# Routing's intermediate values in spare PSUM columns, and the first expert's raw weights loaded four units later

## The chip, the cores and the metric

The kernel runs on one core of a Trainium2 chip. Its engines are TensorE (PE in the profile; PEld is its weight load), VectorE (DVE), ScalarE (ACT), GpSimd (POOL) and SyncE (SP, which only issues DMA transfers here). The metric is the device time of one execution in microseconds (us), as the median of several runs.

## The reference

Three layers follow each other: causal attention over 4 batches, 12 heads, 448 tokens and a head size of 64; a layer of 8 experts, each token going to one; and a dense layer with `h - tanh(h)` between its two products.

```python
scores = scale * np.matmul(q, k.transpose(0, 1, 3, 2))
scores = np.where(mask, -1000000000.0, scores)
attn = np.exp(scores - np.max(scores, axis=-1, keepdims=True))
attn = attn / (np.sum(attn, axis=-1, keepdims=True) + 1e-09)
x = np.matmul(attn, v)                       # (4,12,448,64) -> (1792, 768)

logits = x @ w_gate                          # 8 experts
e_idx = np.argmax(logits, axis=1)
gate_w = softmax(logits)[arange, e_idx]
eom = 1.0 / (1.0 + np.exp(-(x @ w_output_gate)))
for e in range(8):
    out[mask_e] = gate_w * eom[:, e] * (np.maximum(x[mask_e] @ w1[e], 0.0) @ w2[e])

h = out @ w_in
return (h - np.tanh(h)) @ w_out
```

## The kernel before

The program runs the three layers one after the other, with the weights of the next expert loaded and converted meanwhile. Every engine runs its own instructions in the order in which the code writes them down; semaphores make an instruction wait for those of other engines that it depends on. Two engines' uses of one PSUM bank are ordered by such waits too, whichever columns of the bank they touch.

**Attention** is cut into 24 units (NU): unit u is one batch and a pair of heads. A loop runs over u, and inside it over six steps m = 0 to 5 (L607). In each step stand instructions of several units: scores of unit u (`s_mm`, L328 and L329, with the high and the low half of the keys, kh and kl), their row minimum on DVE (`s_max`, L335), the exponential on ACT (`s_exp`), the transposes of unit u-1 (`t_mm`, `t_out`), the product with v of unit u-2 (`v_mm`, L380), its scaling (`v_out`), the split of the result in two 16-bit halves on POOL and its store (`x_out`, `x_store`), the transposes of unit u-3 (`g_mm`, L429) and the router's logits of unit u-4 (`g_lg`, `g_add`). The product with v is made for two heads; head 0 is written in steps 0 to 2 and head 1 in steps 3 to 5. Each head's product lies in one PSUM bank of the pool `ps_o`, which has two banks and is used by the two heads in turn.

**Inputs of the attention.** Two units share one set of inputs, z = u // 2. At step 4 of unit 2z-4, `load_unit(z)` issues a converting load t16 on POOL's queue (L291, `t<-kq` in the trace) and the 32-bit load of q and k and of v on SP's queue (L251, L252, into parts of raw1 or raw2). At step 3 of unit 2z-2, `rest(0)` copies t16 into kh and qa (L300, L301), makes the low half lo for the first unit's heads on POOL (L302) and issues lo's copies into qa and kl (L303, L305); at step 0 of unit 2z-1, `rest(1)` does the second unit's heads. There is one buffer lo, so POOL's L302 of the next z waits for the last kl copy of this z.

**The first expert's w1** has six row blocks k. Block k is loaded into raw1[:, k % 2] on SP's queue at the head of an odd unit (L610) and converted by `conv1` in steps 2 to 4 two units later: two halves on ACT (L115), the rest on POOL (L117 and L131, two of each). The blocks of the second expert's w1 follow into raw1 at units 18 to 23 (`W1_NEXT`, L590).

**Routing** of a batch of 448 tokens begins when the last logits of the batch are summed in `lga`, in step 2 of units 9, 15, 21 and 27. It is a generator whose parts run in steps 0, 2 and 4, each after the attention's instructions of the step: lg (L453, sum of two parts of lga), mx, ex, eq (L462, L463), the one-hot choice oh (L466, L468), the rank among earlier tokens rkm (L495, L496), its quotient and rest pi and pf (L503 to L506), the weight (L473 to L482, with an exponential of es on ACT, L476), and the masks bi, ba and bb for the token list. All these are tiles of [112, 4 to 64] values in the SBUF pool `sm`.

Lines of the change: pools L238 and L239, `v_mm` L371, `routing` L451, `W1_NEXT` L590, the loads L609 and the conversions L671.

Of the kernel before, what the change touches and what calls it, by code (L numbers as in the profile page):

```python
# [12 lines left out]
F32 = mybir.dt.float32  # L13
F16 = mybir.dt.float16
BF16 = mybir.dt.bfloat16
I32 = mybir.dt.int32
# [4 lines left out]
PSUM = bass.MemoryType.PSUM  # L21
SP = mybir.EngineType.SP

B, H, S, D = 4, 12, 448, 64
CP, NCH = 112, 4
NT, DM = B * S, H * D
E, F1 = 8, 1024
F2 = 2048
KD, KF1, KF2 = DM // 128, F1 // 128, F2 // 128
# [30 lines left out]
def build(ctx: ExitStack, tc: tile.TileContext, kq0, kq, v, wg, wo, w1, w2, wf, out):  # L60
    nc = tc.nc
# [33 lines left out]
    raw1 = raw_p.tile([128, KD, F1], F32, name="raw1")  # L95
# [85 lines left out]
    with ExitStack() as actx:  # L181
# [3 lines left out]
        sm = sctx.enter_context(tc.tile_pool(reuse_waits="tile", name="sm", bufs=3, side="right"))  # L185
# [52 lines left out]
        ps_t = actx.enter_context(tc.tile_pool(reuse_waits="tile", name="ps_t", bufs=3, space=PSUM))  # L238
        ps_o = actx.enter_context(tc.tile_pool(reuse_waits="tile", name="ps_o", bufs=2, space=PSUM))  # L239

# [69 lines left out]
        NU = B * 6  # L310
# [60 lines left out]
        def v_mm(u, h, i):  # L371
            d = st_[u]
            hl = (u % 2) * 2 + h
            if ("o", h) not in d:
                d["o", h] = ps_o.tile([128, 512], F32, tag="o", name=f"o_{u}_{h}")[:CP, 0 : NCH * (D + 1)].rearrange(
                    "p (c d) -> p c d", c=NCH)
            po = d["o", h]
            for j in range(i + 1):
                g, o = where[(h, i, j)]
                nc.tensor.matmul(out=po[:, i, :], lhsT=d["PT"][:, g, o : o + CP], rhs=d["t"][3][:, hl, j, :], start=(j == 0),  # L380
                                 stop=(j == i))
# [69 lines left out]
        def routing(b):  # L451
            lg = sm.tile([CP, NCH, 2 * E], F32, tag="lg", name=f"lg_{b}")
            nc.vector.tensor_tensor(out=lg, in0=lga[:, :, 2 * E :], in1=lga[:, :, 0 : 2 * E], op=ALU.add)  # L453
# [6 lines left out]
            nc.scalar.activation(out=ex, in_=ex, func=AF.Exp, scale=1.0 / LSC)  # L460
            eq = sm.tile([CP, NCH, E], F32, tag="eq", name=f"eq_{b}")
            nc.vector.tensor_tensor(out=eq, in0=lg[:, :, 0:E], in1=mxb, op=ALU.is_equal)  # L462
# [8 lines left out]
            def weight():  # L471
                eo = sm.tile([CP, NCH, E], F32, tag="eo", name=f"eo_{b}")
                nc.vector.tensor_tensor(out=eo, in0=lg[:, :, E:], in1=ohb, op=ALU.mult)  # L473
                es = sm.tile([CP, NCH, 1], F32, tag="es", name=f"es_{b}")
                nc.vector.tensor_reduce(out=es, in_=eo, op=ALU.add, axis=AX.X)
                nc.scalar.activation(out=es, in_=es, func=AF.Exp, scale=-1.0 / LSC)  # L476
                sx = sm.tile([CP, NCH, 1], F32, tag="sx", name=f"sx_{b}")
                nc.vector.tensor_reduce(out=sx, in_=ex, op=ALU.add, axis=AX.X)
                yield
                nc.vector.tensor_scalar(out=es, in0=es, scalar1=1.0, scalar2=YSC, op0=ALU.add, op1=ALU.mult)  # L480
                nc.vector.scalar_tensor_tensor(out=es, in0=sx, scalar=1e-9, in1=es, op0=ALU.add, op1=ALU.mult)
                nc.vector.reciprocal(out=tm[:, b * NCH : (b + 1) * NCH, 1:2], in_=es)  # L482
                yield
# [7 lines left out]
            for c in range(NCH):  # L491
                nc.tensor.matmul(out=prv[:, c + 1 :, :], lhsT=onesb[:CP, :CP],
                                 rhs=oh[:, b, c : c + 1, :].to_broadcast([CP, NCH - c, E]), start=False, stop=(c == NCH - 1))
            rk = sm.tile([CP, NCH, E], F32, tag="rk", name=f"rkm_{b}")
            nc.vector.tensor_tensor(out=rk, in0=prv[:, 0:NCH, :], in1=base.unsqueeze(1).to_broadcast([CP, NCH, E]), op=ALU.add)  # L495
# [4 lines left out]
            yield  # L500
            pi = sm.tile([CP, 3, NCH], I32, tag="pi", name=f"pi_{b}")
            pf = sm.tile([CP, 2, NCH], F32, tag="pf", name=f"pf_{b}")
            nc.vector.tensor_copy(out=pi[:, 0, :], in_=rb)  # L503
# [87 lines left out]
        RS, LD = ((3, 0), (0, 1)), (4, 0)  # L591
        W1_NEXT = {NU - KD + j: k for j, k in enumerate((0, 1, 5, 2, 3, 4))}
        CONV = {(NU - 3, 3): (4,), (NU - 2, 3): (5,), (NU - 2, 5): (6,), (NU - 1, 3): (7,), (NU, 3): (0,), (NU, 5): (1,), (NU + 1, 1): (2,), (NU + 1, 4): (3,)}

        def conv1(k, z):
            raw, hi, lo = raw1[:, k % 2], wts0[0][:, 0, k], wts0[0][:, 1, k]
            if z < 2:
                h = slice(512 * z, 512 * (z + 1))
                scaled("a", hi[:, h], raw[:, h])
            else:  # L600
                rest_of("p", lo, raw, hi)
# [5 lines left out]
        for u in range(NU + 5):  # L607
            if ok(u):
                if u % 2 and 3 <= u < 15:  # L609
                    nc.sync.dma_start(out=raw1[:, (u // 2 - 1) % 2], in_=w1[0, :, u // 2 - 1])  # L610
                if u in (8, 10, 12, 14):
# [16 lines left out]
            for m in range(6):  # L628
# [40 lines left out]
                if u == 4 and m == 0:  # L669
                    wts0 = w_tiles(0)  # L670
                if u % 2 and 5 <= u < 17 and 2 <= m < 5:  # L671
                    conv1((u - 5) // 2, m - 2)
                for k in CONV.get((u, m), ()):
# [793 lines left out]
```

## Time and profile before

| what | value |
|---|---|
| median of 3 runs (lowest, highest) | 1032.12 us (1030.98, 1037.31) |
| the profiled execution | 1036.02 us, span 1034.3 us |
| mean granted TensorE clock | 0.982 of full speed |
| PE busy | 981.5 us (95%) |
| DVE, ACT, POOL busy | 785.0, 604.1, 467.3 us |
| attention stage | about 7 to 225 us |

The profile is of one execution. It gives each engine's busy time, the granted clock of TensorE (1.00 is 2.4 GHz, 0.50 is 1.2 GHz), the share of the 16 DMA engines in use, and a timeline in which an instruction that had to wait carries the idle time ahead of it and what ended that time, as `[2.59 <-DMA kl<-lo]`. Times in it count from the span's start.

### The profile page before, as it was taken

What the parts mean: (1) busy time and instruction counts of PE and PEld (TensorE: products, weight loads), DVE (VectorE), ACT (ScalarE), POOL (GpSimd) and SP (SyncE); (2) the same over time, 40 slices, a digit from 0 to 9 for tenths busy, and PEclk for the clock granted to TensorE, in tenths of its full rate; (3) what the DMA queues carried; (4) which work ended last, traced back from release to release, by engine and by line L of the source; (5) the groups of instructions that cost most, each with busy time, mean ns of one, the idle gap of its engine ahead of it and who ended that gap; (6) DMA issues with size and microseconds to landing.
All of it is one profiled execution on the core that took longest, in us unless ns stands there. A gap on an engine that the chain in (4) does not pass through costs nothing. (4 is left out here: it accounts for less than half of the span.)

```text
span 1034.3 us, 23797 instructions
## 1 busy us (share of the span) xinstructions
PE 981.5 (95%) x8985; PEld 735.5 (71%) x8985; DVE 785.0 (76%) x1704; ACT 604.1 (58%) x1213; POOL 467.3 (45%) x504
## 2 busy tenths in 40 slices
PE   5989999999899998998998899999999999999996
PEld 3989999988678786686876455666666666667763
DVE  6647878787887778668886999887888798776640
ACT  5658887765456365564334698565556566555530
POOL 5466776575211021122136689645544443443321
PEclk9979999999999999999999999999999999999999
DMA  8888999954998988988986360010000000000000
GB/s 244 232 200 232 268 263 224 258 188 144 327 338 333 359 277 303 339 295 300 323 321 220 130 273 1 31 40 16 23 32 31 8 32 8 16 16 16 16 24 23
DMA packets 62648, 173.94 MB, mean 168 GB/s; under 512 B 8368, under 2 KB 23344, under 8 KB 59424
## 3 DMA queue, kind: packets, MB, share of 16 engines
q1 hardware_dynamic: 56352, 147.20, 42.5%
q0 software_dynamic: 6144, 24.84, 8.7%
q8 instruction: 80, 1.31, 0.5%
q14 instruction: 72, 0.59, 0.2%
HBM read 132.30 MB, written 29.62 MB: 157 GB/s over the span
## 5 line engine op out<-in xcount | busy, mean ns | idle before, releaser
L1361 PE MATMUL fo<-wo,g 128*128 128x384 f16 x1344 | 228.2, 326 | 0.0
L1310 PEld LDWEIGHTS <-raw 128*128 128x128 f16 x1440 | 141.2, 98 | 86.7 <-issue 9.0
L1361 PEld LDWEIGHTS <-g 128*128 128x128 f16 x1344 | 131.2, 98 | 83.8
L1320 POOL TENSOR_TENSOR V<-cu,cc 128x384 f32<-128x384 f32 (+1 forms) x80 | 80.1, 1001 | 188.0 <-ACT cu L1319 185.4
L164 PEld LDWEIGHTS <-w 128*128 128x128 f16 x2592 | 146.0, 98 | 9.5 <-issue 8.1
L1310 PE MATMUL fh<-cu,raw 128*128 128x384 f16 (+1 forms) x864 | 133.1, 310 | 4.6 <-DVE cc L1318 3.4
L380 PE MATMUL o<-v,PT 112*112 112x65 f32 x960 | 119.4, 266 | 0.0
L343 ACT ACTIVATE P<-s,nb 112x112 f32<-112x112 f32 (+1 forms) x192 | 89.8, 495 | 49.5 <-DVE nb L335 24.9
L380 PEld LDWEIGHTS o<-v,PT 112*112 112x112 f32 x960 | 110.3, 185 | 0.2
L123 DVE SCALAR_TENSOR_TENSOR w<-raw,w 128x768 f16<-128x768 f32 (+1 forms) x99 | 99.0, 1060 | 11.4 <-ACT w L115 11.4
L335 DVE CUSTOM_DVE_ANT_0 s<-s,maskw 112x112 f32<-112x112 f32 (+1 forms) x192 | 85.8, 459 | 21.4 <-PE s L329 18.4
L811 POOL DMA_INDIRECT xg<-xs_d,idx x22 | 30.7, 1397 | 155.9 <-PEq L886 36.5
L1319 ACT ACTIVATE cu<-cc 128x384 f32<-128x384 f32 (+1 forms) x80 | 40.0, 500 | 93.9 <-DVE cc L1318 93.9
L115 ACT ACTIVATE w<-raw 128x768 f16<-128x768 f32 (+2 forms) x106 | 89.4, 904 | 6.7 <-DMA raw<-w 3.9
L1318 DVE TENSOR_TENSOR cc<-fh,co 128x384 f32<-128x384 f32 (+1 forms) x80 | 42.0, 525 | 63.5 <-PE fh L1310 50.8
L1323 POOL TENSOR_TENSOR X<-cc,X 128x384 f32<-128x384 f32 (+1 forms) x80 | 87.6, 1094 | 4.1 <-ACT X L1322 0.5
L1330 DVE SCALAR_TENSOR_TENSOR V<-cu,V 128x384 f32<-128x384 f32 (+1 forms) x80 | 82.6, 1032 | 0.1
L1338 DVE TENSOR_TENSOR V<-V,co 128x384 f32<-128x384 f32 (+1 forms) x64 | 77.5, 1211 | 0.0
L361 PE MATMUL t<-ident,P 112*112 112x112 f32 x480 | 69.3, 268 | 0.0
L1310 PE MATMUL fh<-yh,raw 128*128 128x384 f16 x384 | 67.6, 326 | 0.7 <-DVE cc L1318 0.7
L1339 ACT ACTIVATE g<-V 128x384 f16<-128x384 f32 (+1 forms) x80 | 40.0, 500 | 45.9 <-DVE V L1338 45.7
L328 PE MATMUL s<-kh,qa 128*112 128x112 f16 (+1 forms) x192 | 54.4, 302 | 12.8 <-POOL qa L280 7.3
(670 smaller groups left out, 1978.3 us busy)
## 6 DMA issues: line engine op xcount, KB each, us to landing
raw<-w SPq DMA_DIRECT2D x48, 512.0 KB
raw<-w SPq DMA_DIRECT2D x60, 384.0 KB
cu<-wf SPq DMA_DIRECT2D x22, 1024.0 KB
wb_d<-co SPq DMA_DIRECT2D x22, 512.0 KB
raw<-kq SPq DMA_DIRECT2D x11, 896.0 KB
raw<-wb_d SPq DMA_DIRECT2D x8, 768.0 KB
xs_d<-xq SPq DMA_DIRECT2D x24, 224.0 KB
raw<-v SPq DMA_DIRECT2D x11, 448.0 KB
```

The lines of the kernel that those rows point to most:

```text
L115: nc.scalar.activation(out=out, in_=in_, func=AF.Copy, scale=WS)
L123: nc.vector.scalar_tensor_tensor(out=out, in0=in_, scalar=WS, in1=hi, op0=ALU.mult, op1=ALU.subtract)
L164: nc.tensor.matmul(out=ph[:, (f % 4) * 128 : (f % 4 + 1) * 128], lhsT=w[0][:, ww, k, f * 128 : (f + 1) * 128], rhs=xTs[tag][:, xx, k, :], ...
L335: nc.vector.tensor_tensor_reduce(out=d["s", m][:, z, :], in0=d["s", m][:, z, :], in1=maskw[:, S - n : S], scale=-0.125, scalar=3.0e38, op0 ...
L343: nc.scalar.activation(out=d["P"][:, j, OFF[i] : OFF[i] + n], in_=d["s", m][:, z, :], func=AF.Exp, bias=d["nb"][:, 2 * i + j : 2 * i + j + ...
L380: nc.tensor.matmul(out=po[:, i, :], lhsT=d["PT"][:, g, o : o + CP], rhs=d["t"][3][:, hl, j, :], start=(j == 0), stop=(j == i))
L1310: nc.tensor.matmul(out=ph[:, 0:nt], lhsT=wi[ww][:, f // 4, k, f % 4 * 128 : (f % 4 + 1) * 128], rhs=yy[:, k, 0:nt], start=(q == 0), stop=( ...
L1320: nc.gpsimd.tensor_tensor(out=d["V"], in0=d["U"], in1=d["h"], op=ALU.mult)
L1323: nc.gpsimd.tensor_tensor(out=d["X"], in0=d["h"], in1=d["X"], op=ALU.subtract)
L1330: nc.vector.scalar_tensor_tensor(out=d["V"], in0=d[f"S{z}"], scalar=QD[z - 1], in1=d["V"], op0=ALU.add, op1=ALU.mult)
L1338: nc.vector.tensor_tensor(out=d["V"], in0=d["V"], in1=rs_y(g, nt), op=ALU.mult)
L1361: nc.tensor.matmul(out=po[:, 0:384], lhsT=t[:, x, k, i * 128 : (i + 1) * 128], rhs=wo_[ww][:, k, z * 384 : (z + 1) * 384], start=(k == 0 a ...
```

## The change

The pool `ps_o` gets two fixed tiles, one bank for each head, which are used for the whole attention stage; in the first, columns 320 to 471 hold routing's lg, eq, es, rk, pi and pf, which were SBUF tiles. The six loads of the first expert's w1 are issued at the head of units 7 to 17 instead of 3 to 13, and their conversions in units 9 to 19 instead of 5 to 15. The second expert's row blocks 1 and 5 change places in the order of their loads.

```diff
@@ -236,7 +236,9 @@
-        ps_o = actx.enter_context(tc.tile_pool(reuse_waits="tile", name="ps_o", bufs=2, space=PSUM))
+        ps_o = actx.enter_context(tc.tile_pool(reuse_waits="tile", name="ps_o", bufs=1, space=PSUM))
+        o_ps = [ps_o.tile([128, 512], F32, name=f"o_{h}") for h in range(2)]
+        small = lambda o, n: o_ps[0][:CP, 320 + o : 320 + o + n]
@@ -372,8 +374,7 @@
-                d["o", h] = ps_o.tile([128, 512], F32, tag="o", name=f"o_{u}_{h}")[:CP, 0 : NCH * (D + 1)].rearrange(
-                    "p (c d) -> p c d", c=NCH)
+                d["o", h] = o_ps[h][:CP, 0 : NCH * (D + 1)].rearrange("p (c d) -> p c d", c=NCH)
@@ -449,7 +450,7 @@
-            lg = sm.tile([CP, NCH, 2 * E], F32, tag="lg", name=f"lg_{b}")
+            lg = small(0, NCH * 2 * E).rearrange("p (c e) -> p c e", c=NCH)
@@ -458,7 +459,7 @@
-            eq = sm.tile([CP, NCH, E], F32, tag="eq", name=f"eq_{b}")
+            eq = small(64, NCH * E).rearrange("p (c e) -> p c e", c=NCH)
@@ -471,7 +472,7 @@
-                es = sm.tile([CP, NCH, 1], F32, tag="es", name=f"es_{b}")
+                es = small(128, NCH).unsqueeze(2)
@@ -491,15 +492,15 @@
-            rk = sm.tile([CP, NCH, E], F32, tag="rk", name=f"rkm_{b}")
+            rk = small(96, NCH * E).rearrange("p (c e) -> p c e", c=NCH)
-            pi = sm.tile([CP, 3, NCH], I32, tag="pi", name=f"pi_{b}")
-            pf = sm.tile([CP, 2, NCH], F32, tag="pf", name=f"pf_{b}")
+            pi = small(132, 3 * NCH).bitcast(I32).rearrange("p (a n) -> p a n", a=3)
+            pf = small(144, 2 * NCH).rearrange("p (a n) -> p a n", a=2)
@@ -589,7 +590,7 @@
-        W1_NEXT = {NU - KD + j: k for j, k in enumerate((0, 1, 5, 2, 3, 4))}
+        W1_NEXT = {NU - KD + j: k for j, k in enumerate((0, 5, 1, 2, 3, 4))}
@@ -606,8 +607,8 @@
-                if u % 2 and 3 <= u < 15:
-                    nc.sync.dma_start(out=raw1[:, (u // 2 - 1) % 2], in_=w1[0, :, u // 2 - 1])
+                if u % 2 and 7 <= u < 19:
+                    nc.sync.dma_start(out=raw1[:, (u // 2 - 3) % 2], in_=w1[0, :, u // 2 - 3])
@@ -668,8 +669,8 @@
-                if u % 2 and 5 <= u < 17 and 2 <= m < 5:
-                    conv1((u - 5) // 2, m - 2)
+                if u % 2 and 9 <= u < 21 and 2 <= m < 5:
+                    conv1((u - 9) // 2, m - 2)
```

The order on SP's queue, at the end of unit 2 and in units 3 to 5: the first rows are the low half of the keys (kl) and the 32-bit inputs of the units 6 and 7 (raw<-kq, raw<-v); raw<-w is a block of the first expert's w1, and xs_d a store of a result. Of before:

```order
L305 DMA kl_289<-lo_290 64x896 x2
L251 DMA raw_89<-kq 128x1792
L252 DMA raw_89<-v 112x1024
L610 DMA raw_89<-w 128x1024
L303 DMA qa_287<-lo_290 64x896
L305 DMA kl_289<-lo_290 64x896 x2
L419 DMA xs_d<-xq_531 112x4x256
L419 DMA xs_d<-xq_663 112x4x256
L300 DMA kh_447<-t_3_450 64x1792 x2
L301 DMA qa_446<-t_3_450 64x1792
L303 DMA qa_446<-lo_449 64x896
L305 DMA kl_448<-lo_449 64x896 x2
```

Of the change:

```order
L307 DMA kl_291<-lo_292 64x896 x2
L253 DMA raw_89<-kq 128x1792
L254 DMA raw_89<-v 112x1024
L305 DMA qa_289<-lo_292 64x896
L307 DMA kl_291<-lo_292 64x896 x2
L420 DMA xs_d<-xq_529 112x4x256
L420 DMA xs_d<-xq_659 112x4x256
L302 DMA kh_447<-t_3_450 64x1792 x2
L303 DMA qa_446<-t_3_450 64x1792
L305 DMA qa_446<-lo_449 64x896
L307 DMA kl_448<-lo_449 64x896 x2
```

The row raw<-w is gone from between the inputs and the second half of qa and kl; the other rows keep their order. The same row of unit 5 goes too.

The order on SP's queue at unit 14's end and in unit 15, where the keys of units 16 and 17 (the two halves of kl) are issued. Of before:

```order
L303 DMA qa_1921<-lo_1924 64x896
L305 DMA kl_1923<-lo_1924 64x896 x2
L251 DMA raw_89<-kq 128x1792
L252 DMA raw_89<-v 112x1024
L303 DMA qa_1921<-lo_1924 64x896
L305 DMA kl_1923<-lo_1924 64x896 x2
```

Of the change:

```order
L305 DMA qa_1881<-lo_1884 64x896
L307 DMA kl_1883<-lo_1884 64x896 x2
L253 DMA raw_89<-kq 128x1792
L254 DMA raw_89<-v 112x1024
L611 DMA raw_89<-w 128x1024
L305 DMA qa_1881<-lo_1884 64x896
L307 DMA kl_1883<-lo_1884 64x896 x2
```

Here a block of w1 (raw<-w) now stands ahead of the second half; unit 17 gets one in the same place.

The order on PE in step 1 of unit 11, with what each row waits for in brackets: after the logits of unit 7 (lg), head 0's product with v (o), then the scores of step 2 (s) and their neighbours. Of before:

```order
L441 MATMUL lg_1691<-wgc,xh_1634 112x16
L380 MATMUL o_0_1662<-v_4_957,PT_1475 112x65 x3
L328 LDWEIGHTS qa_1001
L328 MATMUL s_2_1709<-kh_1002,qa_1001 112x336 [waits Activation_49]
L329 LDWEIGHTS qa_1001
L329 MATMUL s_2_1709<-kl_1003,qa_1001 112x336
L361 MATMUL t_2_1712<-ident,P_1473 112x112 [waits Activation_49]
```

Of the change:

```order
L442 MATMUL lg_1654<-wgc,xh_1599 112x16
L381 MATMUL o_172<-v_4_942,PT_1445 112x65 [waits Activation_49]
L381 MATMUL o_172<-v_4_942,PT_1445 112x65 x2
L330 LDWEIGHTS qa_985
L330 MATMUL s_2_1672<-kh_986,qa_985 112x336
L331 LDWEIGHTS qa_985
L331 MATMUL s_2_1672<-kl_987,qa_985 112x336
L363 MATMUL t_2_1675<-ident,P_1443 112x112 [waits PE_49]
```

The first product with v of the step now waits for ACT, whose instruction on es lies in the same bank; the wait that stood at the scores is covered by it. The same stands in units 17 and 23, and in step 1 of units 10, 16 and 22 that product waits for DVE.

## Rows read from the trace of the kernel before

**Rows 1.** The page: busy time of engines, and granted clock (tenths) in 40 slices.

```profile
PE 981.5 (95%) x8985; PEld 735.5 (71%) x8985; DVE 785.0 (76%) x1704; ACT 604.1 (58%) x1213; POOL 467.3 (45%) x504
...
PEclk9979999999999999999999999999999999999999
```

**Rows 2.** Windows: us, busy per engine (instructions), granted clock, DMA share, GB/s.

```profile
45.00:50.00 5.00, 5.00 (x53) 4.68 (x53) 3.96 (x16) 3.23 (x8) 1.84 (x3) 1.00 1.07 319
54.40:61.20 6.80, 4.74 (x48) 4.29 (x48) 3.22 (x13) 5.28 (x11) 6.46 (x8) 1.00 0.94 251
61.20:68.00 6.80, 6.27 (x41) 6.09 (x41) 2.68 (x12) 2.64 (x9) 2.14 (x4) 0.50 0.88 214
68.00:74.90 6.90, 6.90 (x36) 6.24 (x35) 2.62 (x11) 2.61 (x5) 5.36 (x5) 0.50 0.80 175
```

**Rows 3.** Timeline of PE: start us, us, instruction xcount [idle before <-releaser].

```profile
58.93 0.21 PE L328 MATMUL s<-kh,qa 128*112 128x112 f16 x1
61.73 0.25 PE L329 MATMUL s<-kl,qa 128*112 128x112 f16 x1 [2.59 <-DMA kl<-lo]
...
76.16 0.21 PE L328 MATMUL s<-kh,qa 128*112 128x112 f16 x1
...
84.46 0.21 PE L328 MATMUL s<-kh,qa 128*112 128x112 f16 x1
```

**Rows 4.** Timeline of SP, units 3 and 4: transfers as they are issued.

```profile
38.50 0.52 SPq L610 DMA_DIRECT2D raw<-w  x1
...
39.63 1.31 SPq L305 DMA_DIRECT2D kl<-lo  x2
...
52.82 1.85 SPq L305 DMA_DIRECT2D kl<-lo  x2
```

**Rows 5.** Timeline of POOL, units 4 and 5.

```profile
50.39 1.89 POOL L302 TENSOR_TENSOR lo<-raw,t 128x896 f16<-128x896 f32 x1 [3.40 <-DMA kl<-lo]
...
52.81 0.58 POOL L291 DMA_DIRECT2D t<-kq  x1
```

**Rows 6.** DMA issues of the first 80 us: count, KB each.

```profile
raw<-w SPq DMA_DIRECT2D x3, 512.0 KB
```

**Rows 7.** Timelines of PEld and PE: two later waits.

```profile
136.04 0.13 PEld L329 LDWEIGHTS <-qa 128*112 128x112 f16 x1 [0.72 <-DMA kl<-lo]
...
276.29 4.18 PE L164 MATMUL ph_I-6030_6031<-xT_n,w 128*128 128x128 f16 x72 [1.89 <-PEq L886]
```

**Rows 8.** Timeline of POOL, units 15 to 17.

```profile
150.92 0.62 POOL L117 TENSOR_SCALAR sca<-raw 128x512 f32<-128x512 f32 x1
151.62 1.16 POOL L131 TENSOR_TENSOR w<-sca,w 128x512 f16<-128x512 f32 x1
...
158.04 1.88 POOL L302 TENSOR_TENSOR lo<-raw,t 128x896 f16<-128x896 f32 x1
...
167.25 0.62 POOL L408 TENSOR_SCALAR xq<-xt 112x512 f16<-112x512 f32 x1 [3.70 <-ACT xt L402]
```

**Rows 9.** Timeline of DVE: routing of the second and the last batch.

```profile
157.46 2.51 DVE L496 TENSOR_TENSOR rkm<-rkm,oh 112x32 f32<-112x32 f32 x1
...
162.34 0.72 DVE L503 CAST pi<-rank 112x4 int32<-112x4 f32 x1
...
244.81 0.19 DVE L496 TENSOR_TENSOR rkm<-rkm,oh 112x32 f32<-112x32 f32 x1
...
245.26 0.17 DVE L503 CAST pi<-rank 112x4 int32<-112x4 f32 x1
```

**Rows 10.** Timeline of PE: the first matmul of units 16 and 18.

```profile
152.63 0.21 PE L328 MATMUL s<-kh,qa 128*112 128x112 f16 x1
...
170.94 0.21 PE L328 MATMUL s<-kh,qa 128*112 128x112 f16 x1
```

**Rows 11.** Timelines of PE and ACT in unit 17.

```profile
164.12 0.78 PE L380 MATMUL o<-v,PT 112*112 112x65 f32 x6
...
165.66 0.20 ACT L476 ACTIVATE es<-es 112x4 f32<-112x4 f32 x1
```

## The prediction

> **What bounds the kernel now.** I read the page first: TensorE (PE) is busy for 95% of the span [rows 1], so a change pays only where PE stands still or where its clock is halved. The clock line of the page has one dip inside the attention stage, in its third slice [rows 1]. The windows put numbers on it: the granted clock is 1.00 up to 61.2 us and 0.50 (the lower of the two levels, 1.2 GHz) in both windows between 61.2 and 74.9 us [rows 2]. The timeline of PE then says what came ahead of the fall: unit 6 of the attention starts at 58.93 us, its second matmul comes at 61.73 us, and PE sat idle for 2.59 us before it, waiting for the DMA of kl, the low half of the keys [rows 3]. Unit 7 starts at 76.16 and unit 8 at 84.46 us [rows 3]. So unit 6 lasted 17.23 us where unit 7 lasted 8.30: 8.93 us were lost, 2.59 of them idle and 6.34 to the halved clock.
>
> Why were the keys late? SP's timeline shows the order of its transfers: raw<-w, 512 KB of the first expert's weights, was issued at 38.50 us, ahead of the second half of unit 4's and 5's keys (kl at 39.63) [rows 4, 6]. GpSimd (POOL) could begin the next low half (lo) only when that kl had landed and freed the one lo buffer; it waited 3.40 us and began at 50.39 [rows 5]. SP issued unit 6's kl from it at 52.82 [rows 4], and it landed at 61.73 [rows 3]. From 45 to 50 us the DMA engines' share was 1.07 [rows 2]: they were full, so each kilobyte ahead of those keys delayed them.
>
> **The change part by part.**
>
> *Two weight loads leave units 3 and 5.* The one at 38.50 us lay ahead of the keys that gated lo. Its price is 524 kB at the rate of the moment: 1.6 us at the 319 GB/s of the window from 45 to 50 us, 2.1 us at the 251 GB/s of the window just ahead of the fall [rows 2]. I take 2.0, nearer the slower, since the transfer must have finished on the slowest engine. Then lo begins at 48.4 instead of 50.39, SP issues kl at 50.8, and it lands at 59.7 instead of 61.73. PE is ready for it at 58.93 + 0.21 = 59.14 [rows 3]. What is left of the wait is about 0.6 us (0.5 to 1.0 by the two rates). It is 0 if the load in unit 5, which also goes, held back the last packets of this kl; it is 2.59 again if the transfer t<-kq, which POOL issues on its own queue at 52.81 [rows 5], was the whole cause.
>
> Does 0.6 us keep the clock? Rows of this kernel say so: PE's waits of 0.72 us at 136 and 1.89 us at 276 were followed by no fall, while the 2.59 us here was [rows 1, 2, 7]. So unit 6 should take 8.3 + 0.6, and the term is −8.93 + 0.6 = **−8.3 us**.
>
> *Two loads arrive in units 15 and 17.* Now the keys of units 16 and 18 come behind a weight load, as those of units 10 to 14 had before; and units 8 and 9, no longer preceded by a slow stretch in which the DMA engines caught up, come under the same regime. The worst wait for kl under that load is the 0.72 us at 136 [rows 7]. Three such places cost between 0 and 2.2 us; I take **+0.8**, a third of the bound, since one alone of those earlier pairs showed such a wait.
>
> *Conversions move by four units* (2 instructions of ScalarE, ACT, and 4 of POOL in each of six units). They leave units 5 and 7 and arrive in 17 and 19. POOL's four take 2 × (0.62 + 1.16) = 3.6 us by the rows at 150.92, and in unit 17 POOL sat idle 3.70 us ahead of its xq at 167.25 [rows 8]: hidden, 0. Uncovered, POOL would be 3.6 us late with the next xq and lo, and kl with it. The swap of rows 1 and 5 in the next expert's loads keeps each load behind its buffer's last reader: 0.
>
> *Routing's values move to PSUM.* In the trace the same VectorE (DVE) instruction is short or long: L496, 112x32, takes 0.19 us at 244.81 and 2.51 us at 157.46, and the long one lies beside POOL's 1.88 us lo instruction at 158.04; L503 took 0.72 us at 162.34, beside the next lo, and 0.17 in the last batch [rows 8, 9]. Both read SBUF alone, and both will have an operand in PSUM. The Trainium skill (SBUF — State Buffer, "Who interferes with whom") says that a DVE instruction with two SBUF inputs, or a copy in a two-port mode, contends with GpSimd, and one with at most one SBUF input does not; by that rule lg (L453), which still adds two parts of lga from SBUF, stays long at times, and the others become short. The trace agrees as far as it goes; no run so far shows these operations on PSUM.
>
> What of it reaches PE? Unit 16 starts at 152.63 and unit 18 at 170.94 [rows 10]: the two units took 18.31 us, 1.71 over twice 8.30, and L496's 2.51 us lies in the first of them. I take **−1.0**, between 0 (DVE's delay is hidden anyway) and −1.7.
>
> *New waits.* The bank that now holds routing's values is that of the first head's output, which PE writes in the first half of every unit. The order in the section on the change shows PE waiting for ACT's instruction on es where it had no wait. In unit 17 of before that instruction started at 165.66 us and took 0.20, and PE's matmul had started at 164.12 [rows 11]: 1.74 us of wait if nothing else moves, and behind PE's matmul everything of the unit is queued. But DVE came late to es because of L496 and L503, which by the last paragraph lose 2.3 and 0.6 us, more than those 1.74. I take **+0.2**, between 0 and 5.2 (1.74 in each of three batches). The Trainium skill (PSUM — Partial Sum Buffer, "PSUM bank collisions raise a hardware error") has a rule against this change: two engines must be kept apart by bank, whatever the columns. The waits in the order agree with it. By it alone, without shorter DVE work, the sum would be worse by that bound; this is the third rival.
>
> *Sum:* −8.3 + 0.8 − 1.0 + 0.2 = −8.3 us. Everything behind the attention stage starts earlier by the same amount: weights are loaded when their buffers come free, so the loads shift along. The profiled execution took 1036.02 us (span 1034.3) and would take 1027.7. The median of the three timed runs is 1032.12, 3.9 us lower; I subtract from it: 1023.8 us.
>
> **The rivals.**
>
> 1. *The wait only moves* (chance 0.16). kl stays over 2 us late at unit 6, or comes so at unit 8, since t<-kq shares the engines with it, and the clock falls all the same. For it: t<-kq was issued within 0.01 us of kl [rows 4, 5]. Against it: at the later pairs the same two transfers meet, with weights behind them, and only 0.72 us was lost [rows 7]. What remains is routing's 1.0: 1031.1 us.
> 2. *The change does less than it says* (0.12). The timed runs pay 3.9 us less than the profiled one; if that is a part of unit 6's loss, only 8.3 − 3.9 = 4.4 us are to be gained: 1027.7. For it: the profiled time lies near the top of the timed ones (1030.98 to 1037.31); against it: one of those is above it.
> 3. *Slower: PE waits for routing* (0.06). If DVE stays late, PE waits 1.74 us in each of three batches, and where one such wait passes 1.89 us the clock may fall again, for 6.3: −8.3 + 0.8 + 5.2 + 6.3 = +4.0, so 1036.1. It decides from the point where es starts 1.7 us or more behind PE's matmul.
> 4. *More* (0.14). No wait is left at unit 6, none arrives later, and routing gives its whole 1.7: −8.93 − 1.7 = −10.6, so 1021.5.
>
> The forecast holds 0.52.
>
> **How the numbers follow.** The likeliest case gives 1023.8 us. The range, 1019.5 to 1031.5, takes in the first, second and fourth rival and the bounds of the terms, with 2 us below the fourth for the spread of a median of three; it leaves out the third and the tails. One per cent, 10.3 us, is about what a measurement of this kernel can tell from no change. Faster by more than that needs under 1021.8: most of the fourth rival, 0.12, and the better end of the forecast, 0.08, so 0.20. Slower by more needs over 1042.4, which is the third rival with a second fall of the clock: 0.04. The rest, 0.76, is within 1%, though I expect a gain there.
>
> **What would show it.** In the new profile: PE's wait for kl at about 59 us under 1 us; the granted clock 1.00 from 31 us to the end of the attention; unit 8 starting near 76 us instead of 84.46; L496 and L503 near 0.19 us in every batch while lg is still long in places; waits of PE for ACT's es under 0.5 us; kl waits under 1 us at units 16 and 18. I am wrong if a window of clock 0.50 stands between 60 and 225 us, if unit 8 starts later than 80 us, or if PE idles for es by more than 1 us.

## The result, and the profile after

The changed kernel is faster, by more than forecast in the first comparison and by about as much as forecast in the second, and for another reason than the one forecast. In the first comparison its median was 1020.49 us (1016.43 to 1024.17, 6 runs) against 1034.79 us of the kernel before (1030.98 to 1037.31, 6 runs): 14.3 us less, ratio 0.9866, 95% interval 0.9834 to 0.9898. In a later one it was 1021.75 us (12 runs) against 1029.05 us (31 runs): 7.3 us less, ratio 0.9951, interval 0.9921 to 0.9981. Ratios leave out runs over 1.5% above the fastest of their kernel, which are more often runs of before.

The forecast was 1023.8 us. The profiled execution took 1022.38 us (span 1020.6) where before's took 1036.02 (span 1034.3).

The page after, beside [rows 1]: PE is busy for 10.6 us less, and the clock line has no dip inside the attention, nor at its start.

```profile
PE 970.9 (95%) x8985; PEld 727.1 (71%) x8985; DVE 775.7 (76%) x1704; ACT 604.2 (59%) x1213; POOL 460.7 (45%) x504
...
PEclk9999999999999999999998999999999999999998
```

The windows of after, at the places of [rows 2] (us, busy time of each engine, granted clock, DMA share, GB/s): the clock is 1.00 in all four.

```profile
45.00:50.00 5.00, 5.00 (x54) 4.69 (x52) 3.96 (x16) 3.28 (x8) 4.55 (x6) 1.00 0.85 214
54.40:61.20 6.80, 6.80 (x80) 6.50 (x78) 4.30 (x20) 5.81 (x15) 0.75 (x1) 1.00 1.01 279
61.20:68.00 6.80, 6.80 (x74) 6.49 (x73) 5.00 (x20) 4.73 (x11) 4.81 (x6) 1.00 0.90 220
68.00:74.90 6.90, 6.90 (x78) 6.58 (x77) 5.16 (x21) 5.19 (x16) 4.26 (x5) 1.00 0.98 261
```

The timeline of PE after, for [rows 3]: units 6, 7 and 8 start at 58.76, 67.12 and 75.42 us. Unit 6 takes 8.36 us, and kl is there when PE comes to it.

```profile
58.76 0.21 PE L330 MATMUL s<-kh,qa 128*112 128x112 f16 x1
58.83 0.26 PE L331 MATMUL s<-kl,qa 128*112 128x112 f16 x1
...
67.12 0.21 PE L330 MATMUL s<-kh,qa 128*112 128x112 f16 x1
...
75.42 0.21 PE L330 MATMUL s<-kh,qa 128*112 128x112 f16 x1
```

Routing's instructions on DVE after, for [rows 9]. The columns are: line, operation, count, least, median and largest ns of one, first and last start. The product that took up to 2.51 us (now L497) and the conversions (L504 to L507) are short in all four batches; lg (L454), which still adds two parts from SBUF, is not.

```profile
L497 DVE TENSOR_TENSOR o<-o,oh x4: 198/199/200, 98.1 to 235.5; 112x32 f32<-112x32 f32 x4
```

```profile
L507 DVE CAST o<-o x4: 174/174/174, 101.9 to 236.5; 112x8 f32<-112x8 int32 x4
```

```profile
L454 DVE TENSOR_TENSOR o<-lga x4: 636/808/1173, 88.1 to 232.6; 112x64 f32<-112x64 f32 x4
```

The waits of PE after, from 80 to 225 us (us in total, times, longest): none is for ACT's es.

```profile
PE s L331 <- DMA kl<-lo: 1.9, 3, 1.1
PE xt L430 <- POOL xq L410: 0.7, 3, 0.3
```

Read alone, this pair of traces confirms the forecast: the wait for kl has gone, the clock stays up, and unit 8 starts 9.0 us earlier. The experiments say otherwise.

### The profile page after: what moved, and what is told of

It is laid out like the page before. It is cut to its first block, busy times and chain, and to the rows that moved or that the text cites. A ratio compares the mean times of both kernels' runs of the same rounds, so it can differ in the third digit from the quotient of the medians.

```text
span 1020.6 us, 23802 instructions
## 1 busy us (share of the span) xinstructions
PE 970.9 (95%) x8985; PEld 727.1 (71%) x8985; DVE 775.7 (76%) x1704; ACT 604.2 (59%) x1213; POOL 460.7 (45%) x504
## 5 line engine op out<-in xcount | busy, mean ns | idle before, releaser
L164 PEld LDWEIGHTS <-w 128*128 128x128 f16 x2592 | 145.9, 98 | 10.3 <-issue 9.1
L1311 PE MATMUL fh<-cu,raw 128*128 128x384 f16 (+1 forms) x864 | 136.0, 315 | 3.4 <-DVE cc L1319 2.2
L381 PE MATMUL o<-v,PT 112*112 112x65 f32 x960 | 114.6, 259 | 0.0
L381 PEld LDWEIGHTS o<-v,PT 112*112 112x112 f32 x960 | 105.4, 178 | 0.2
L812 POOL DMA_INDIRECT xg<-xs_d,idx x22 | 25.7, 1170 | 154.8 <-PEq L887 30.1
L1324 POOL TENSOR_TENSOR X<-cc,X 128x384 f32<-128x384 f32 (+1 forms) x80 | 90.8, 1135 | 4.2 <-ACT X L1323 0.5
L363 PE MATMUL t<-ident,P 112*112 112x112 f32 x480 | 67.0, 262 | 0.0
L330 PE MATMUL s<-kh,qa 128*112 128x112 f16 (+1 forms) x192 | 53.3, 294 | 12.7 <-POOL qa L282 7.5
```

The costliest lines, as they stand in the source:

```text
L164: nc.tensor.matmul(out=ph[:, (f % 4) * 128 : (f % 4 + 1) * 128], lhsT=w[0][:, ww, k, f * 128 : (f + 1) * 128], rhs=xTs[tag][:, xx, k, :], ...
L1311: nc.tensor.matmul(out=ph[:, 0:nt], lhsT=wi[ww][:, f // 4, k, f % 4 * 128 : (f % 4 + 1) * 128], rhs=yy[:, k, 0:nt], start=(q == 0), stop=( ...
L1324: nc.gpsimd.tensor_tensor(out=d["X"], in0=d["h"], in1=d["X"], op=ALU.subtract)
```

## The experiments

The theories. **A**, the forecast's: the two weight loads ahead of the keys cause the late keys and the fall of the clock at unit 6. **N**: routing's instructions on DVE, held beside POOL's, delay DVE, then ACT, then PE, and PSUM ends this. **C**: what differs between the two first traces is partly the chance of one execution. Two more letters, B and H, stand in the expectations of psum_only and of lo_split and mean what is said there.

All timed runs, with two numbers worked out from each run's span and mean granted clock. Work is span × clock, an estimate of the span had PE run at full clock throughout. Clock loss is span × (1 − clock). Both are means over the runs that the ratio uses.

| kernel | routing in PSUM | median us (range, runs) | before beside it | ratio, 95% interval | work | clock loss |
|---|---|---|---|---|---|---|
| changed, first | all | 1020.5 (1016.4–1024.2, 6) | 1034.8 | 0.9866 [0.9834, 0.9898] | 1009.9 | 8.8 |
| after_again | all | 1021.8 (1017.9–1033.7, 12) | 1029.1 | 0.9951 [0.9921, 0.9981] | 1009.1 | 10.8 |
| psum_only | all, old loads | 1021.8 (1019.8–1026.0, 4) | 1029.9 | 0.9878 [0.9792, 0.9963] | 1011.7 | 8.9 |
| psum_again | all, old loads | 1022.4 (1016.2–1026.8, 12) | 1029.1 | 0.9940 [0.9909, 0.9971] | 1011.1 | 9.2 |
| load3_5 | all, two more loads | 1023.3 (1020.4–1030.2, 10) | 1029.9 | 0.9927 [0.9885, 0.9969] | 1010.2 | 12.0 |
| lg_psum | all, and lg's input | 1020.9 (1019.0–1022.8, 8) | 1029.1 | 0.9918 [0.9885, 0.9951] | 1008.9 | 10.3 |
| psum_b01 | batches 0, 1 | 1024.1 (1019.6–1031.8, 12) | 1032.4 | 0.9941 [0.9906, 0.9975] | 1011.8 | 11.7 |
| psum_b2 | batch 2 | 1032.1 (1023.7–1037.0, 12) | 1029.1 | 1.0043 [1.0011, 1.0076] | 1014.2 | 16.0 |
| pipf_only | pi, pf | 1032.3 (1022.9–1039.3, 12) | 1032.4 | 1.0017 [0.9978, 1.0057] | 1012.5 | 14.8 |
| no_pipf | all but pi, pf | 1035.2 (1024.6–1049.7, 13) | 1032.4 | 1.0039 [1.0007, 1.0071] | 1014.9 | 16.6 |
| loads_only | none, new loads | 1029.5 (1023.1–1041.0, 10) | 1029.9 | 1.0009 [0.9966, 1.0051] | 1013.8 | 14.3 |
| b_again | none | 1032.4 (1023.8–1048.2, 10) | 1029.9 | 0.9992 [0.9946, 1.0037] | 1016.3 | 12.7 |
| lo_split | none | 1043.8 (1035.1–1053.2, 10) | 1032.4 | 1.0116 [1.0076, 1.0155] | 1019.4 | 21.2 |

The runs of before beside them (22, 24 and 31 used) had a work of 1014.4, 1014.5 and 1015.2 us and a clock loss of 12.9, 12.2 and 13.9 us. The standard error of these means is 0.5 to 1.5 us, that of the clock loss of pipf_only 2.1. How far two lots of runs of one kernel can differ is seen in b_again: its work of 1016.3 us stands against 1014.4 of the runs of before beside it, so a difference under 2 us in these columns says little.

### b_again: the kernel before, once more

> The kernel before, unchanged, run and profiled once more. The changed kernel gained 14.3 us (1034.8 to 1020.5), 9.3 us of it inside the attention and 5 to 6 us more near 410 us, where PE of before stood still for 1.97 us (behind ACT's hh) and then ran at clock 0.50 from 409.4 to 416.2 us. Theory A (the stall at 409 us is a part of this kernel's order of events): the second profile has a stall of over 1 us and a window of clock 0.50 between 400 and 420 us again. Theory C (it is a chance of one execution): no such window there in the second profile, and the mean clocks of its timed runs spread by more than 0.005. Both expect unit 6's wait for kl of over 2 us at 59 us and the half clock from 61 to 75 us again, and a time of 1031 to 1037 us. The half clock from 23.7 to 30.5 us of before has no counterpart in the changed kernel: if it is a chance, it is missing in some of these.

It had neither the wait at unit 6 (unit 6 lasted 8.30 us) nor a stall at 409 us, so both belong to one execution. PE's waits for kl from 12 to 215 us (us in total, times, longest):

```profile
PE s L329 <- DMA kl<-lo: 1.4, 3, 0.7
```

But its clock fell elsewhere in the attention, from 106.4 to 113.2 us, and here the timelines of DVE, POOL, ACT and PE in unit 11 show the chain that the forecast had missed.

```profile
101.28 1.86 DVE L504 TENSOR_SCALAR pi<-pi 112x4 int32<-112x4 int32 x1
103.06 0.16 DVE L505 TENSOR_SCALAR pi<-pi 112x4 int32<-112x4 int32 x1
103.25 3.01 DVE L506 CAST pf<-pi 112x8 f32<-112x8 int32 x1
106.16 0.62 DVE L335 CUSTOM_DVE_ANT_0 s<-s,maskw 112x448 f32<-112x448 f32 x1
...
101.23 1.89 POOL L302 TENSOR_TENSOR lo<-raw,t 128x896 f16<-128x896 f32 x1 [2.49 <-DMA xs_d<-xq]
103.09 0.61 POOL L306 TENSOR_SCALAR v<-raw 112x512 f32<-112x512 f32 x1
103.65 0.59 POOL L291 DMA_DIRECT2D t<-kq  x1
104.27 1.89 POOL L302 TENSOR_TENSOR lo<-raw,t 128x896 f16<-128x896 f32 x1
...
106.87 0.63 ACT L343 ACTIVATE P<-s,nb 112x448 f32<-112x448 f32 x1 [4.50 <-DVE nb L335]
...
107.56 0.44 PE L328 MATMUL s<-kh,qa 128*112 128x336 f16 x1 [3.00 <-ACT P L343]
```

```profile
99.60:106.40 6.80, 4.96 (x61) 4.72 (x60) 6.69 (x12) 2.31 (x4) 5.14 (x5) 1.00 0.86 203
106.40:113.20 6.80, 5.64 (x28) 5.05 (x28) 5.35 (x27) 5.51 (x16) 3.77 (x5) 0.50 1.03 320
```

L504 works on 4 elements in each partition, takes 0.17 us in the last batch, and here ends 0.02 us after POOL's first lo. pf, on 8 elements, begins at 103.25 and ends at 106.26, 0.10 us after the second lo. The row minimum of the next scores (L335) stands behind it on DVE; ACT's exponential waited 4.50 us for that, PE stood still for 3.00 us (104.56 to 107.56) for ACT, and in that wait PE's clock went to 0.50 (1.2 GHz), where it stayed for 6.8 us. The Trainium skill (SBUF — State Buffer, "Who interferes with whom") calls what DVE and GpSimd share an exclusive lock, under which the later one fully blocks. The row of L504 agrees: it began 0.05 us after POOL's lo. The row of pf agrees only in part: it began during POOL's v, but was still held when v had ended, and the second lo, which began 1.02 us after pf, went ahead of it.

### psum_only, loads_only: each half alone

```diff
 psum_only (from the changed kernel; the loads, and not shown here the conversions and W1_NEXT, as before)
-                if u % 2 and 7 <= u < 19:
+                if u % 2 and 3 <= u < 15:
 loads_only (from the kernel before; not shown: the conversions and W1_NEXT as in the changed kernel)
-                if u % 2 and 3 <= u < 15:
+                if u % 2 and 7 <= u < 19:
```

> Routing's values in PSUM and the fixed output tiles as in the changed kernel, the weights' loads and conversions in their old units. Theory A (the late keys at unit 6 come from the weight load ahead of them; PSUM only shortens DVE's work by 1 us): 1033.8 us, 1 us under before, unit 6 still waits over 2 us for kl and the clock is 0.50 from 61 to 75 us. Theory B (routing in PSUM carries the 5 us that the forecast missed): 1029 us. If PE waits for ACT's es by 1.74 us in each of three batches: 1039 us.

> The weights' loads and conversions in their new units, routing's values in SBUF and the output tiles from the pool as before. Theory A: 9 to 13 us under before, so 1022 to 1026 us: PE waits under 1 us at unit 6, and no clock of 0.50 between 60 and 225 us. Theory B: 1026 us, since PSUM's part is missing; then psum_only is at 1029. Where the two parts simply add up, this run's gain and that of psum_only add to 14.3 us.

Theory A is out. The moved loads alone change nothing that can be told (0.4 us by the medians, the interval includes 1), and PSUM alone gives 8.1 us: more than theory B's 5. The times that A and B gave for the two runs were all missed, in part because the median of before was itself 1029.9 us here and not 1034.8. With the weights in their old units psum_only has no long wait for kl at unit 6 either (0.23 us there). PE's waits for kl from 12 to 215 us:

```profile
PE s L331 <- DMA kl<-lo: 1.8, 5, 0.5
```

loads_only shows what stays by chance: its clock fell at the start of the attention, in unit 3, before any routing.

```profile
33.00:46.60 13.60, 13.50 (x73) 12.52 (x74) 5.32 (x22) 5.21 (x14) 7.22 (x7) 0.50 0.92 232
```

### load3_5: the two loads brought back

```diff
+                if u in (3, 5):
+                    nc.sync.dma_start(out=raw1[:, (u // 2 - 1) % 2], in_=w1[0, :, u // 2 - 1])
                 if u % 2 and 7 <= u < 19:
```

> The changed kernel with two more loads of 512 KB into the still unused raw1, at the start of units 3 and 5, where before loaded its first weights; no conversion comes with them, and what they load is loaded over later. Theory A (the transfer ahead of the keys is the cause): the wait for kl at unit 6 is 2 us or more again, the clock is 0.50 for some 13.7 us behind it, and the time is 1029 us, 8.9 us over the changed kernel. Rival (ACT's and POOL's conversions in unit 5 delayed lo and so the keys): 1020.5 us as the changed kernel, PE waits under 1 us.

Neither the wait nor the fall came back; over the whole attention PE's longest wait for kl was 0.5 us. The time, between the two that were expected, lies 1.5 to 2.8 us over the changed kernel's, nearly all of it in the clock loss; whether those loads cause that is not settled.

### after_again, psum_again: the pair on one chip

> The changed kernel once more, beside the kernel before and psum_again on one chip. Theory N (routing in PSUM makes the gain, by shortening DVE's instructions beside POOL's; the moved loads give little): 1020 to 1022 us, within 2 us of psum_again. Theory A (the moved loads save the stall at unit 6): 5 us or more under psum_again. In the profile both expect 19.3 us from unit 23 to the first expert's first matmul, 25.8 us from unit 16 to 19.

> Routing in PSUM with the weights' loads in their old units, once more (the first four runs gave 1021.8 us). Theory N: 1021 to 1023 us, 8 us under before, with the clock loss (span times one less the mean clock) at 9 us where before loses 13. Theory A: 1026 us or more, and the profile shows PE waiting over 2 us for kl at unit 6.

The two medians differ by 0.7 us, against 6.6 and 7.3 us from before, and by the ratios (0.9951 and 0.9940) the kernel without the moved loads gains as much. So what the loads are worth can't be told from nothing, and PSUM brings the gain.

### psum_b2, psum_b01: which batch

```diff
-            lg = small(0, NCH * 2 * E).rearrange("p (c e) -> p c e", c=NCH)
+            lg = small(0, NCH * 2 * E).rearrange(...) if b == 2 else sm.tile([CP, NCH, 2 * E], F32, ...)
 ... (eq, es, rk, pi, pf alike; b < 2 in psum_b01)
```

> The changed kernel with routing in PSUM for the third batch alone (b == 2), the others in SBUF as before. Theory N in its parts: the stretch from unit 23 to the first expert's first matmul, beside which the third batch's routing runs, takes 19.3 us as in the changed kernel (21.2 in before), and unit 16 to 19 takes 26.8 to 27.4 us as in before (25.8 in the changed kernel); the time lies 2 to 4 us over the changed kernel, 1023 to 1025 us. Rival (the fixed output tiles or the place in memory make the gain, not routing's instructions): as the changed kernel in every stretch, 1020 to 1022 us.

> The changed kernel with routing in PSUM for the first two batches, and in SBUF for the third and the fourth. psum_b2, with the third batch alone in PSUM, gave 1032 us, so the first two should carry most of the gain: 1023 to 1025 us; from unit 23 to the first expert's first matmul 21.2 us as in before (19.3 in the changed kernel), unit 16 to 19 under 26.3 us as in the changed kernel. Rival (each batch gives a third): 1026 to 1028 us.

The third batch's share is seen in the traces, in the stretch from unit 23 to the first expert's first matmul, here for the changed kernel (19.27 us) and b_again (21.08):

```profile
205.48 0.21 PE L330 MATMUL s<-kh,qa 128*112 128x112 f16 x1
...
224.75 0.33 PE L164 MATMUL ph_first<-xT_n,w 128*128 128x128 f16 x3
```

```profile
210.95 0.21 PE L328 MATMUL s<-kh,qa 128*112 128x112 f16 x1
...
232.03 0.33 PE L164 MATMUL ph_first<-xT_n,w 128*128 128x128 f16 x3
```

psum_b2 has 19.26 us there, psum_b01 21.08. In psum_b01 two waits for DVE stand in it that the changed kernel has not:

```profile
PE px L531 <- DVE bb L522: 0.8, 1, 0.8
PE xt L430 <- DVE xq L419: 0.3, 1, 0.3
```

That gain of the stretch does not show in psum_b2's timed runs, though: their work is 1014.2 us against 1014.5 of before beside them, their clock loss 16.0 against 12.2, and the median isn't under that of before. The first two batches carry most of the gain: with them in PSUM the median is 8.2 us under before, and the ratio (0.9941) is that of all batches.

Three expectations failed. psum_b2 was to take 1023 to 1025 us and took 1032.1. Its profile shows 25.86 us from unit 16 to 19, as short as with PSUM, where 26.8 to 27.4 were expected; but that profiled run, at 1023.65 us, was the fastest of its twelve. In psum_b01 the same stretch took 26.33 us where under 26.3 was expected. A single profile doesn't show what the other runs lose; the mean clocks of psum_b2's twelve (0.977 to 0.992) say that they lose it to falls of the clock, and where these lie is not on record.

### pipf_only, no_pipf: which instructions

```diff
 pipf_only: lg, eq, rk and es back in SBUF
-            eq = small(64, NCH * E).rearrange("p (c e) -> p c e", c=NCH)
+            eq = sm.tile([CP, NCH, E], F32, tag="eq", name=f"eq_{b}")
 no_pipf: pi and pf back in SBUF
-            pf = small(144, 2 * NCH).rearrange("p (a n) -> p a n", a=2)
+            pf = sm.tile([CP, 2, NCH], F32, tag="pf", name=f"pf_{b}")
```

> The changed kernel with only pi and pf in PSUM; lg, eq, rk and es in SBUF as before. If the conversions on pi and pf (112x4 and 112x8, one input each, up to 3.01 us in a profile of before) make the stalls of PE: 1021 to 1024 us, within 2 us of the changed kernel. If the additions and products with two inputs in SBUF (eq, rk, eo) make them: 1027 us or more.

> The changed kernel with pi and pf back in SBUF; lg, eq, rk and es stay in PSUM. If the conversions on pi and pf make the stalls: 1027 us or more, with instructions of 1.8 us or longer on pi or pf in the profile. If those with two inputs in SBUF make them: 1021 to 1024 us.

Each was expected to be fast if the other was slow; by the medians neither is faster than before. In work pipf_only lies in between (1012.5 us, against 1015.2 of before and 1008.9 to 1011.7 with all routing in PSUM), but its clock loss is that of before. Both have the fixed output tiles, as psum_b2 has, so those alone don't bring the gain. In pipf_only the conversions are all at 0.17 us, but eq takes up to 1.12 us, rkm 1.56 and eo 1.05, as before; its profile is that of the fastest of its twelve runs, without a fall of the clock in the attention, so how the others lose their time isn't seen. no_pipf shows something else: the forecast's third rival. Its es lies in PSUM, its pi and pf in SBUF. In unit 11 (timelines of DVE and POOL, windows, and PE's waits from 95 to 112 us):

```profile
101.09 1.71 DVE L504 CAST pi<-rank 112x4 int32<-112x4 f32 x1
102.84 3.07 DVE L505 TENSOR_SCALAR pi<-pi 112x4 int32<-112x4 int32 x1
...
102.74 0.62 POOL L308 TENSOR_SCALAR v<-raw 112x512 f32<-112x512 f32 x1
103.30 0.58 POOL L293 DMA_DIRECT2D t<-kq  x1
103.92 1.89 POOL L304 TENSOR_TENSOR lo<-raw,t 128x896 f16<-128x896 f32 x1
```

```profile
105.70:115.90 10.20, 7.20 (x36) 6.62 (x37) 6.53 (x30) 5.82 (x16) 5.98 (x8) 0.50 1.03 310
```

```profile
PE o L381 <- ACT o L477: 4.6, 1, 4.6
```

DVE came late to es, PE stood 4.6 us behind ACT's instruction on the shared bank, and the clock was at 0.50 for 10.2 us; the same again in the second batch, with 3.7 us. That execution took 1045.0 us, the second longest of thirteen, so it shows the mechanism and not how often it strikes. So with es in PSUM a late conversion makes PE wait, and by the medians only all the values together gain.

### lg_psum: lg's input as well

```diff
+                nc.vector.tensor_tensor(out=lga[:, :, 0 : 2 * E], in0=lga[:, :, 0 : 2 * E], in1=plg[:, :, 0 : 2 * E], op=ALU.add)
+                nc.vector.tensor_tensor(out=lgp, in0=lga[:, :, 2 * E :], in1=plg[:, :, 2 * E :], op=ALU.add)
...
-            nc.vector.tensor_tensor(out=lg, in0=lga[:, :, 2 * E :], in1=lga[:, :, 0 : 2 * E], op=ALU.add)
+            nc.vector.tensor_tensor(out=lg, in0=lgp, in1=lga[:, :, 0 : 2 * E], op=ALU.add)
```

> The changed kernel, with lg's first input in PSUM too: the last addition to lga of a batch is made in two halves, of which the upper goes to the PSUM columns that eq and rk use later, so lg adds one part from PSUM and one from SBUF. If two inputs in SBUF are what makes an instruction of DVE wait beside POOL: lg, 112x64, falls from 0.64 to 1.17 us to under 0.3 us in the first three batches, and the time is 0 to 1.5 us under the changed kernel. If it is the size or the place in the program: lg stays at 0.6 us or more, and the time stays.

lg falls to 0.23 us in every batch:

```profile
L459 DVE TENSOR_TENSOR o<-o,lga x4: 231/232/232, 88.3 to 231.2; 112x64 f32<-112x64 f32 x4
```

So two inputs in SBUF are what holds it. The median, 0.9 us under after_again, can't be told from it; the range is the narrowest of all (3.8 us).

### lo_split: POOL's instruction in eight

```diff
-                nc.gpsimd.tensor_tensor(out=lo[:, hs], in0=t32[:, hs], in1=t16[:, hs], op=ALU.subtract)
+                for h in (2 * y, 2 * y + 1):
+                    for n in range(0, S, S // 4):
+                        ns = slice(n, n + S // 4)
+                        nc.gpsimd.tensor_tensor(out=lo[:, h, ns], in0=t32[:, h, ns], in1=t16[:, h, ns], op=ALU.subtract)
```

> The kernel before (routing in SBUF, weights in their old units), with POOL's lo instruction of 128x896 made as eight of 128x112, each of about an eighth of 1.89 us and some start-up. Theory H (a DVE instruction of routing is held until the POOL instruction beside it has ended): DVE's longest routing instruction, 3.01 us in the second profile of before (pf, 112x8, beside lo's 1.89 us), falls under 0.8 us, PE's waits behind it go, and the time comes 4 to 8 us under before, 1021 to 1025 us. Rival S (the two engines share a port evenly while both are at work, whatever the length of one instruction): pf and pi still take 1.8 to 3.0 us, and the time is that of before or above, since POOL's start-ups add work.

11.4 us slower than before. Theory H holds only here and there. Timelines of DVE and POOL in unit 11:

```profile
105.09 0.39 DVE L506 CAST pi<-rank 112x4 int32<-112x4 f32 x1
105.50 0.32 DVE L507 TENSOR_SCALAR pi<-pi 112x4 int32<-112x4 int32 x1
105.74 0.44 DVE L508 TENSOR_SCALAR pi<-pi 112x4 int32<-112x4 int32 x1
106.21 4.07 DVE L509 CAST pf<-pi 112x8 f32<-112x8 int32 x1
...
103.27 2.88 POOL L305 TENSOR_TENSOR lo<-raw,t 128x112 f16<-128x112 f32 x8 [1.53 <-DMA raw<-w]
106.12 0.62 POOL L309 TENSOR_SCALAR v<-raw 112x512 f32<-112x512 f32 x1
106.68 0.58 POOL L291 DMA_DIRECT2D t<-kq  x1
107.29 2.87 POOL L305 TENSOR_TENSOR lo<-raw,t 128x112 f16<-128x112 f32 x8
```

Beside the first eight pieces (0.36 us each) each conversion is held for about one piece, 0.32 to 0.44 us. But pf, which began during POOL's v, was held for 4.07 us through v, the issue of t<-kq and all eight pieces of the next lo, and ended 0.12 us after the last. In b_again the 3.01 us began during v too. So did pi's 3.07 us in no_pipf. Pieces are no sure opening either: in unit 9 of lo_split lg, with two inputs in SBUF, was held for 2.73 us, through six of them and v.

```profile
90.34 2.73 DVE L456 TENSOR_TENSOR lg<-lga 112x64 f32<-112x64 f32 x1
...
89.44 2.87 POOL L305 TENSOR_TENSOR lo<-raw,t 128x112 f16<-128x112 f32 x8
92.29 0.61 POOL L309 TENSOR_SCALAR v<-raw 112x512 f32<-112x512 f32 x1
```

What decides whether DVE is let in between two instructions of POOL stays open. The eight also cost POOL 1.0 us more for each lo (2.88 for 1.89), and PE then waits 5.6 us in all for xq, and up to 2.5 us at a time for ACT's P, in the attention.

## Why the prediction was right in size and wrong in cause

The time fell inside the range, and that is luck: the −8.3 us stood for a stall that other executions of before do not have, and what brought the gain is routing, forecast at −1.0. The steps come out as follows.

**Unit 6, −8.3 us: wrong.** The rows were read rightly, and the mechanism may be that of this one execution; no run shows it a second time. Of the kernels with weight loads in units 3 and 5, five more profiles (b_again, psum_only, psum_again, load3_5, lo_split) have no wait over 0.7 us for kl from 12 to 215 us, and no fall at unit 6; in b_again unit 6 lasted 8.30 us, so there was nothing to be gained. The step that failed is the one that took a stall found once as the kernel's property. The second rival touched it, by setting the profiled time against the timed ones, with a chance of 0.12. Theory A's own trace, before against after, looked like proof; it was two draws.

**Loads to units 15 and 17, +0.8: not shown.** In the first pair of traces PE's waits for kl from 80 to 225 us grew from 0.6 to 1.9 us, but most of it at unit 10 (1.09 us at 93.3) and none over 0.3 us at units 16 and 18; after_again, the same kernel, has 0.2 us in all, less than before. **Conversions moved, order swapped, 0:** loads_only agrees, within its interval of 0.4%.

**Routing, −1.0: too small, by a factor of about four in work alone.** I had counted one batch, the second, and taken its 1.71 us as the upper bound for all. The stages, with half-clock time counted half, give (means of before, b_again and loads_only, against the two profiles each of the changed kernel and of psum_only, and load3_5):

| stretch | SBUF us | PSUM us | gain |
|---|---|---|---|
| unit 9 to 12 (batch 0) | 27.05 (25.7–27.9) | 26.13 (25.3–26.7) | 0.9 |
| unit 16 to 19 (batch 1) | 27.07 (26.8–27.4) | 25.91 (25.3–26.7) | 1.2 |
| unit 23 to first expert (batch 2) | 21.19 (21.1–21.3) | 19.29 (19.3–19.3) | 1.9 |

That is 4.0 us, an estimate: only batch 2's gain is clear of the spread between executions. In batches 0 and 1 the two columns overlap or nearly do, and psum_b2, with both in SBUF, has 25.91 and 25.86 us there. The work in the table of runs fell by about as much (1014.4 to 1015.2 for before, 1009.1 to 1011.7 with all routing in PSUM). The rest is clock loss: 12 to 14 us in before, 9 to 12 with PSUM. Falls of the clock behind a late DVE are a cost that this term had put at nothing. b_again and no_pipf show how such a fall comes behind a late DVE; in how many executions of before it does so isn't shown, since only one run of each kernel has a trace.

**PE behind es, +0.2: right, with its condition.** No wait for es stands in the changed kernel, so the term was 0. The reason given, that DVE is no longer late, is borne out by no_pipf: with two of the values left in SBUF PE waits 4.6 and 3.7 us, more than the 1.74 us at which the rival set its price. The rival was a real edge.

**All behind the attention shifts along: not as traced.** The gain between the first two traces grew from 9.3 us at 276 us to 14.5 us at 421 us, because before had waited 1.97 us for ACT's hh at 409 us and run at half clock behind it; b_again had not. psum_only, psum_again, load3_5, lg_psum and psum_b01 have a fall of their own that begins between 424 and 427 us, each in or just behind a wait of PE of 2.8 to 5.6 us for ACT's xT_n; neither profile of the changed kernel has that. So what happens behind the attention differs from execution to execution, and a pair of traces can't price it.

**The checks that I named** (clock 1.00 to the end of the attention, unit 8 near 76 us, short L496 and L503, long lg, no wait for es) all came true in the first trace. They could not tell theory A from N, because the trace of before held both losses, and the changed kernel removed one and happened not to have the other.

## What to carry to other kernels

A stall in one profile is a sample: before pricing it, set the mean clock and span of every timed run beside the profiled one, and take a second profile of the unchanged kernel. Small values in PSUM keep DVE free beside a busy POOL, but here it paid only when nearly the whole chain went (lg's two inputs stayed); a chain half moved made PE wait at the bank for the half left behind. When a hazard appears in several batches, count each of them and ask which engine stands behind the late one in each.

## What the runs showed of the hardware

Which DVE instructions of routing are held beside POOL goes by their operands, not their size. In the traces with routing in SBUF, those with two SBUF inputs were long at times (rkm<-rkm,oh 2.75 us in b_again, eo 1.78 in loads_only, eq 1.16 in before, for 0.16 to 0.19 beside an idle POOL), and so were conversions and scalar operations with one SBUF input and an SBUF output (pi 1.86 and pf 3.01 in b_again, es 0.87 in before). Never long were rkm<-rk,base and base<-base,rk, whose second input is in PSUM (0.19 and 0.15 us in every batch; 17 of the 25 rkm<-rk,base began while POOL was at work), and the reductions (up to 0.19). In the trace of before a short one and a long one stand side by side, both begun within one instruction of POOL: the next row on DVE is the 2.51 us of [rows 9], which began 0.58 us before that instruction's end and lasted until lo ended too.

```profile
157.23 0.19 DVE L495 TENSOR_TENSOR rkm<-rk,base 112x32 f32<-112x32 f32 x1 [0.40 <-PE rk L492]
...
156.88 1.16 POOL L409 TENSOR_TENSOR xq<-xt,xq 112x512 f16<-112x512 f32 x1
```

That is the division that the Trainium skill makes (SBUF — State Buffer, "Who interferes with whom"). Not expected was that a held instruction of 4 or 8 elements can outlast three of POOL's instructions (b_again 3.01 us, no_pipf 3.07), and is not surely let in between short ones (lo_split, 4.07 us). Cutting POOL's work into pieces was the wrong remedy here.
